# Hash attention and a Strassen SwiGLU block on one core: sums in another bank, weight words four pieces ahead, later gates, key before query

## The chip, the core and the metric

The kernel runs on one core of a Trainium2 chip. Five engines work beside each other, each in the order of its own queue: PE (TensorE, matrix products), DVE (VectorE), ACT (ScalarE), POOL (GpSimd, here the issuer of most transfers) and SP (SyncE, issuer of the others). The metric is device microseconds (us) of one execution.

## The reference

```python
def _attn_ref(q, k, v, proj):            # (4, 8, 768, 64), proj (64, 6)
    q_bucket = sum over 6 bits of (q @ proj > 0) * 2**bit
    k_bucket = the same of k
    scores = where(q_bucket == k_bucket, q @ k.T / 8, -1e9)
    attn = softmax(scores)               # with 1e-9 added to the sum
    return attn @ v

def _moe_ref(x, w_gate, w_val, w_out):   # (3072, 512), (512, 1536) twice, (1536, 512)
    g = x @ w_gate
    return (g * sigmoid(g) * (x @ w_val)) @ w_out
```

The attention's output, with its 8 heads side by side, is the x of the second block. Inputs are float32, apart from the three weights: these come as 64-bit doubles, as two 32-bit words each, and the kernel turns them into float32 itself.

## The kernel before

**Attention.** A batch has 4 pairs of heads; 4 batches make 16 pairs. A pair is done in two halves of 384 queries. I call such a half of a pair a unit and number the units 0 to 31; units 0 to 7 are the first batch's. In a unit `score` (L464) does six chunks of 128 keys for two heads: a float32 product of 64 rows, and a bfloat16 product of hash signs added on top in the same bank, which pushes pairs of unlike hash far down. ACT evicts each with an exponential (L467) into a ring of six tiles. `attend` (L476) multiplies them with the values into one bank of PSUM that has a pool of its own (`av_ps`, one buffer), and ACT copies it out (L480). `add` (L487, L491) sums the exponentials on DVE, `norm` (L501) adds up over the keys with a product by ones into a bank of the common pool, and DVE does a reciprocal (L504) and two more operations (L506, L507). The common pool `ps` has seven banks in rotation, for scores, transposes, hashes, sums and the feed-forward's products.

Ahead of a pair its queries and keys are transposed and hashed (`front`): in the first batch by PE (L388, L405), with ACT as evictor; later by DVE's block transposes (L431) and small hash products (L413). For pair 0 the order of these steps is written out by hand in `front`, and the first five of the eight are done before the first score.

**Weights.** 36 pieces of 128 x 512 doubles are brought in (`load_words`, L261), scaled by two ACT instructions (`scale_to`, L286 and L287) and put together on DVE in three steps (`narrow`, L303, L305, L308). Of each block of four pieces `form` makes, with eight DVE steps (L337), the combinations that Strassen's method wants, and writes them to a scratch in HBM (L330, L332, L339); `bring` (L322) reads them back when they are used. All of this is one generator, `preparing`, and `prepare_on(n)` takes n DVE steps from it at chosen places in the program. `load_words(i)` is called at the end of piece i and issues the loads of the next ones: up to four ahead for the first twelve pieces, three ahead afterwards. The words live in five tiles inside the hidden layer's buffer, idle at that time, for the first twelve pieces, and then in three tiles. `scale_ahead` lets ACT scale up to three (later two) pieces ahead. Piece 0 also has a check of the word order, with five DVE instructions more (L282 to L285, L300, L310).

**Feed-forward.** Once a batch's attention is complete, its feed-forward is cut into parts (`atoms`), which are put behind the attention of the next batch's units, about fourteen to a unit. An up stage (`both`) has seven Strassen products for the gate and seven for the value in turn (L533), on six banks named a, b and c. The first three are copied out by ACT (L591); for the later ones DVE adds the bank to what is there (L537). Then the gate: a tanh on ACT (L519), a first DVE step (L520), and for the value branch a second (L524), each of them one part after the product. Beside each part, 0.7 DVE steps of `preparing` and one `scale_ahead` are done. The down stage (`down_strassen`) does likewise with banks named po.

Each engine's queue has the order in which these calls are written out: nothing reorders them later.

Of the kernel before, what the change touches and what calls it, by code (L numbers as in the profile page):

```python
# [18 lines left out]
def kernel(  # L19
# [219 lines left out]


    words = {}
    EARLY = 12

    def as_words(t):
        return t.bitcast(I32).rearrange("p (f w) -> p f w", w=2)

    spare = hid.rearrange("p a b f q -> p (a b f q)")
    spare = [as_words(spare[:, i * 2 * PIECE : (i + 1) * 2 * PIECE]) for i in range(5)]
    beside = as_words(part(2 * PIECE, at=down_at + 8 * BL))

    def load_words(done, queue=nc.gpsimd):
        for i in range(len(words), len(pieces)):
            if i - done > (4 if i < EARLY else 3):
                break
            if i < EARLY:
                words[i] = spare[i % 5]
            elif i % 3 == 2:
                words[i] = beside
            else:
                words[i] = wraw.tile([P, PIECE, 2], I32, tag="words", name="words")  # L260
# [4 lines left out]
    bits_a, bits_b = (formed[x].rearrange("p n m -> p (n m)").bitcast(I32)[:, 0:PIECE]  # L265
                      for x in range(2))

    def scale_to(count):

        free = NJ * (progress["blocks"] + 2)
        if free >= 2 * NJ * DF // PIECE:
            free = len(pieces)
        for i in range(progress["scaled"], min(count, free, len(pieces))):
            t, w = words[i], pieces[i][0]
            top = t.rearrange("p f w -> p (f w)").bitcast(U16)
            top = top.rearrange("p (f w) -> p f w", w=4)[:, :, 1]
            if i == 0:

# [5 lines left out]
            nc.scalar.activation(w, t[:, :, 1].bitcast(FP32), AF.Copy, scale=2.0**-112)  # L286
            nc.scalar.activation(t[:, :, 0], top, AF.Copy, scale=2.0**-13 * (1 + 2.0**-17))  # L287
            progress["scaled"] = i + 1

    def scale_ahead():  # L290
        i = progress["piece"]
        scale_to(i + (3 if i < EARLY - 2 else 2))

    def narrow(i):
# [3 lines left out]
        wi = w.bitcast(I32)  # L298
        if i == 0:
            nc.vector.tensor_tensor(bits_b.bitcast(FP32), bits_a, lo, op=ALU.not_equal)  # L300
        scale_to(i + 1)
# [6 lines left out]
        nc.vector.tensor_tensor(wi, wi, lo, op=ALU.add)  # L308
        if i == 0:
            nc.vector.scalar_tensor_tensor(out=w, in0=bits_b.bitcast(FP32), scalar=1e4, in1=w,  # L310
                                           op0=ALU.mult, op1=ALU.add)
        progress["piece"] = i + 1
# [67 lines left out]
    def front(n):  # L380
# [158 lines left out]
    def up_strassen(x, b, first):  # L539
# [14 lines left out]
        def both(i):  # L554
# [4 lines left out]
            now = [{}, {}]  # L559
            later = {}  # L560

# [6 lines left out]
            def step(at):  # L568
# [34 lines left out]
                if at == 13:  # L603
                    later.pop(14)()

# [100 lines left out]

    prepare_pair(5)
    finish(rest)
    N = len(units)
    credit = ahead = 0.0  # L710
    for u in range(0, N, NCH):
# [41 lines left out]
        credit += 14 if n < 2 * NP else 15.75  # L753
        end = True
        while atoms and (credit > 0 or not end):
# [48 lines left out]
```

The softmax here doesn't subtract the row's maximum and nothing guards it: scores larger than these inputs give would overflow.

## Time and profile before

| what | before |
|---|---|
| time, median of 3 runs | 1030.21 us (1028.72 to 1030.33) |
| span of the profiled run | 1028.6 us |
| ACT busy | 418.8 us, 41% |
| POOL busy | 99.3 us, 10% |
| moved by DMA | 99.90 MB, mean 97 GB/s |

A line of the groups gives source line, engine, operation, output and input, count, busy time and mean, and then the idle time of the engine just before these instructions with what ended it:

```profile
L504 DVE RECIPROCAL r<-sum 128x384 f32<-128x384 f32 x32 | 81.7, 2554 | 27.1 <-PE sum L501 27.1
L467 ACT ACTIVATE A<-sc 128x384 f32<-128x384 f32 x256 | 105.9, 492 | 7.9 <-PE sc L464 7.8
L591 ACT COPY c<-up 128x384 f32<-128x384 f32 x72 | 34.4, 478 | 70.9 <-PE up L533 70.7
```

The first of them: 32 reciprocals of 2554 ns each, before which DVE idled for 27.1 us in all until the sums of PE were there. Idle time of an engine that isn't the bottleneck costs nothing. The row of 40 slices puts the work in time; a slice is 25.7 us:

```profile
DVE  5999987869895445565656472565656451525521
ACT  6776647365452413544352421534435201232200
```

### The profile page before, as it was taken

To read this page: it belongs to the slowest core of one execution; us is meant where nothing else is said; L and a number is where in the kernel's file an instruction comes from. 1 tells how busy PE (TensorE), PEld (TensorE's weight loads), DVE (VectorE), ACT (ScalarE), POOL (GpSimd) and SP (SyncE) were. 2 spreads that over 40 slices of the span, in tenths; PEclk is the share of its full clock that TensorE was granted. 3 is DMA by queue.
4 is the path that set the end of the run, shared out by engine and by line. 5 is a ranking of instruction groups with operands and counts; after the bars stand their busy time and mean duration, and the time that the engine had idled before them with its cause. 6 is when DMAs were issued, how large, how long until landed. Compare 5 with 4: busy or idle time off the path is not lost.

```text
span 1028.6 us, 12425 instructions
## 1 busy us (share of the span) xinstructions
PE 1014.7 (99%) x4597; PEld 610.6 (59%) x4597; DVE 624.5 (61%) x1012; ACT 418.8 (41%) x905; POOL 99.3 (10%) x192
## 2 busy tenths in 40 slices
PE   9999999999999999999999999999999999999998
PEld 4444455555557775555556677555555787555687
DVE  5999987869895445565656472565656451525521
ACT  6776647365452413544352421534435201232200
POOL 2212022321100000000000000000000000101000
PEclk9999999999999999999999999999999999999999
DMA  7656485744622114242321203233222000333101
GB/s 212 196 163 201 120 216 203 212 162 156 172 72 52 37 31 107 72 103 82 84 81 37 62 21 93 59 82 95 72 72 72 21 21 31 109 97 113 31 26 36
DMA packets 113884, 99.90 MB, mean 97 GB/s; under 512 B 86976, under 2 KB 97216, under 8 KB 113824
## 3 DMA queue, kind: packets, MB, share of 16 engines
q0 software_dynamic: 19104, 73.28, 21.7%
q1 hardware_dynamic: 93920, 25.64, 11.3%
q8 instruction: 36, 0.59, 0.2%
q10 hardware_dynamic: 800, 0.20, 0.1%
q14 instruction: 24, 0.20, 0.1%
HBM read 81.79 MB, written 17.30 MB: 96 GB/s over the span
## 4 chain that ended last, share of the span: by engine, by line
PE 81%; DVE 10%; issue 4%; DMA 3%; ACT 2%; POOL 1%; DVEq 0%; POOLq 0%
PE up L533 36%; PE po L533 21%; PE sc L464 11%; PE av L476 9%; DVE acc L491 2%; DMA words<-in_moe_w_out_dram 2%; DVE r L504 2%; PE sum L501 1%; DVE room L305 1%; PE hps L413 1%; DVE room L337 1%; DVE room L308 1%; ACT A L467 1%; PE hps L405 1%; DVE room L303 1%
## 5 line engine op out<-in xcount | busy, mean ns | idle before, releaser
L533 PE MATMUL up<-xT,room 128*128 128x384 f32 x768 | 263.5, 489 | 0.0
L533 PEld LDWEIGHTS up<-xT,room 128*128 128x128 f32 x768 | 143.9, 190 | 109.7 <-issue 15.2
L533 PE MATMUL up<-xc,room 128*128 128x384 f32 x576 | 198.3, 487 | 2.0 <-ACT hid L591 1.5
L464 PE MATMUL sc<-qT,kT 64*128 64x384 f32 x768 | 164.3, 498 | 7.3 <-DVE e L506 3.3
L533 PEld LDWEIGHTS up<-xc,room 128*128 128x128 f32 x576 | 109.0, 190 | 79.8 <-ACT hid L591 2.8
L537 DVE TENSOR_TENSOR c<-c,up 128x384 f32<-128x384 f32 x72 | 39.8, 552 | 151.9 <-PE up L533 151.9
L491 DVE TENSOR_TENSOR acc<-acc,A 128x768 f32<-128x768 f32 x128 | 122.7, 958 | 14.6 <-ACT A L467 1.6
L322 POOL DMA_DIRECT2D room<-ram x96 | 52.0, 542 | 671.9 <-PE up L533 662.4
L467 ACT ACTIVATE A<-sc 128x384 f32<-128x384 f32 x256 | 105.9, 492 | 7.9 <-PE sc L464 7.8
L464 PEld LDWEIGHTS sc<-qT,kT 64*128 64x128 f32 x768 | 69.6, 188 | 62.9 <-issue 45.5
L661 ACT COPY o<-po 128x256 f32<-128x256 f32 x48 | 17.9, 372 | 199.2 <-PE po L533 199.1
L504 DVE RECIPROCAL r<-sum 128x384 f32<-128x384 f32 x32 | 81.7, 2554 | 27.1 <-PE sum L501 27.1
L476 PE MATMUL av<-A,vraw 128*64 128x386 f32 x512 | 88.4, 487 | 0.0
L519 ACT ACTIVATE th<-c 128x384 f32<-128x384 f32 x72 | 37.6, 522 | 104.4 <-DVE c L537 104.2
L537 DVE TENSOR_TENSOR o<-o,po 128x256 f32<-128x256 f32 x36 | 15.2, 421 | 102.2 <-PE po L533 61.1
L467 ACT ACTIVATE room<-sc 128x384 f32<-128x384 f32 x128 | 54.3, 488 | 38.6 <-PE sc L464 38.3
L533 PE MATMUL po<-wo,hid 128*128 128x256 f32 x288 | 66.9, 382 | 0.0
L464 PE MATMUL sc<-qb,kb 64*128 64x384 bf16 x384 | 66.7, 324 | 0.2 <-DVE kb L400 0.2
L533 PE MATMUL po<-wo,room 128*128 128x256 f32 x288 | 66.3, 380 | 0.0
L533 PE MATMUL po<-room,hid 128*128 128x256 f32 x288 | 66.1, 379 | 0.0
L476 PEld LDWEIGHTS av<-A,vraw 128*64 128x64 f32 x512 | 36.8, 137 | 46.2 <-issue 45.3
L591 ACT COPY c<-up 128x384 f32<-128x384 f32 x72 | 34.4, 478 | 70.9 <-PE up L533 70.7
(113 smaller groups left out, 1041.3 us busy)
## 6 DMA issues: line engine op xcount, KB each, us to landing
room<-ram POOLq DMA_DIRECT2D x48, 512.0 KB, 4.7
room<-ram POOLq DMA_DIRECT2D x48, 384.0 KB, 3.9
vraw<-in_v_dram SPq DMA_DIRECT2D x16, 384.0 KB, 3.2
ram<-room POOLq DMA_DIRECT2D x12, 512.0 KB, 4.1
out_dram<-o SPq DMA_DIRECT2D x48, 128.0 KB, 1.7
qraw<-in_q_dram SPq DMA_DIRECT2D x48, 96.0 KB, 3.2
kraw<-in_k_dram SPq DMA_DIRECT2D x46, 96.0 KB, 3.4
words<-in_moe_w_out_dram POOLq DMA_DIRECT2D x8, 512.0 KB, 4.7
```

Of the source, the lines that this page charges most:

```text
L303: nc.vector.tensor_single_scalar(wi, wi, 3, op=ALU.logical_shift_left)
L322: nc.gpsimd.dma_start(places[k % 2][:, PARTS[go], :], ram[k % NG][:, PARTS[go], :])
L464: nc.tensor.matmul(sc[h], x["k", n][rows, ks], x["q", n][rows, qs], start=start, stop=not start)
L467: nc.scalar.activation(weights(u)[:, h, 0:HQ], sc[h], AF.Exp, scale=SCALE)
L476: nc.tensor.matmul(ps[h * D : (h + 1) * D, 0:AW], raws["v", n][:, h, c, :], a[:, h, :], start=c == 0, stop=c == NCH - 1)
L491: nc.vector.tensor_tensor(acc[n, half], acc[n, half], a[:, :, 0:HQ], op=ALU.add)
L504: nc.vector.reciprocal(r, ps[:, 0:HQ])
L519: nc.scalar.activation(th, g, AF.Tanh, scale=0.5)
L533: nc.tensor.matmul(ps, a, x, start=start and i == 0, stop=i == len(pairs_) - 1, skip_group_check=True)
L537: nc.vector.tensor_tensor(o, a, b, op=op)
L591: nc.scalar.copy(tile_of(g, spot), c)
L661: nc.scalar.copy(o, c)
```

## The change

It has five parts. The sums of the first batch's units go into the value product's bank instead of one of the seven. Words are loaded four pieces ahead throughout and scaled three ahead, in more tiles that lie in space idle at that time: the front and then the back of the hidden layer's buffer, and then the staging area; in the feed-forward's units the scaling is done only beside the parts after the fifth, and one preparation step beside each of the first ten parts. In the first batch four of the eight preparation steps of a unit move behind the reciprocal. The gate's second step, and its first, come two parts after the product instead of one. For pair 0 the key's first half is transposed and hashed ahead of the query's, and its second half behind the first score. The check of piece 0 is dropped. The purpose is to take waits out of the queues of ACT and DVE and to free PSUM banks of the rotation.

```diff
-    EARLY = 12
-    spare = hid.rearrange("p a b f q -> p (a b f q)")
-    spare = [as_words(spare[:, i * 2 * PIECE : (i + 1) * 2 * PIECE]) for i in range(5)]
-    beside = as_words(part(2 * PIECE, at=down_at + 8 * BL))
+    spots = [hid[:, half, m].rearrange("p f q -> p (f q)") for half in range(2) for m in range(2)]
+    early = [as_words(t[:, 0 : 2 * PIECE]) for t in spots]
+    early.append(as_words(part(2 * PIECE, at=down_at + 8 * BL)))
+    middle = [as_words(t[:, NFP // 2 * HQ : NFP // 2 * HQ + 2 * PIECE]) for t in spots]
+    late = [as_words(part(2 * PIECE, at=stage_at + i * 2 * PIECE)) for i in range(4)]
+
+    def words_tile(i):
+        if i < 12:
+            return early[i % 5]
+        if i < 24 and i % 6 < 4:
+            return middle[i % 6]
+        if i >= 24 and i % 6 not in (2, 3):
+            return late[i % 6 // 4 * 2 + i % 2]
+        return wraw.tile([P, PIECE, 2], I32, tag="words", name="words")
...
-            if i - done > (4 if i < EARLY else 3):
+            if i - done > 4:
                 break
...
-            if i == 0:
-                nc.vector.tensor_single_scalar(bits_a, t[:, :, 0], 29, op=ALU.logical_shift_right)
-                nc.vector.tensor_scalar(bits_b, t[:, :, 0], scalar1=28, scalar2=1,
-                                        op0=ALU.logical_shift_right, op1=ALU.bitwise_and)
-                nc.vector.tensor_tensor(bits_a, bits_a, bits_b, op=ALU.add)
...
-        scale_to(i + (3 if i < EARLY - 2 else 2))
+        scale_to(i + 3)
...
-            return [turns[2], turns[0], turns[1], hashes[2], hashes[0], hashes[1], turns[3],
+            return [turns[0], turns[2], hashes[0], hashes[2], turns[1], hashes[1], turns[3],
                     hashes[3]]
...
-        ps = bank("sum")
+        ps = av_ps.tile([P, 512], FP32, tag="av", name="sum") if b == 0 else bank("sum")
...
+                while later and later[0][0] <= at:
+                    later.pop(0)[1]()
                 if n >= 3 and g == 0:
-                    later[at + 1] = gate(tile_of(0, spot) if n == 6 else c, c)
+                    then = gate(tile_of(0, spot) if n == 6 else c, c)
                 elif n >= 3:
-                    later[at + 1] = lambda: gated(hidden(f + spot[0], spot[1]), now[0][spot], c)
-                if at in later:
-                    later.pop(at)()
+                    then = lambda: gated(hidden(f + spot[0], spot[1]), now[0][spot], c)
+                if n >= 3:
+                    later.append((at + (1 if n == 6 else 2), then))
...
-    prepare_pair(5)
+    prepare_pair(4)
...
-            if u == 0 and c in (1, 2, 4):
+            if u == 0 and c in (0, 1, 2, 4):
...
-        prepare_on(2 if u == LATE else 6)
+        prepare_on(2)
         norm(u + NCH - 1)
+        prepare_on(0 if u == LATE else 4)
...
             atom()
-            ahead += 0.7 * size
-            prepare_on(int(ahead))
-            ahead %= 1
-            scale_ahead()
+            part += size
+            if part < 11:
+                prepare_on(size)
+            if part > 5:
+                scale_ahead()
```

More of the change, by code (lines that the diff above doesn't have):

```diff
@@ L241 @@
     words = {}
-    EARLY = 12
     def as_words(t):
         return t.bitcast(I32).rearrange("p (f w) -> p f w", w=2)
-    spare = hid.rearrange("p a b f q -> p (a b f q)")
-    spare = [as_words(spare[:, i * 2 * PIECE : (i + 1) * 2 * PIECE]) for i in range(5)]
-    beside = as_words(part(2 * PIECE, at=down_at + 8 * BL))
+    spots = [hid[:, half, m].rearrange("p f q -> p (f q)") for half in range(2) for m in range(2)]
[11 more added lines that the diff above has]
+        return wraw.tile([P, PIECE, 2], I32, tag="words", name="words")
     def load_words(done, queue=nc.gpsimd):
         for i in range(len(words), len(pieces)):
-            if i - done > (4 if i < EARLY else 3):
+            if i - done > 4:
                 break
[L255 to L260, printed above, removed]
+            words[i] = words_tile(i)
             queue.dma_start(words[i].rearrange("p f w -> p (f w)"), pieces[i][1])
     progress = {"late": False, "piece": 0, "scaled": 0, "blocks": 0}
-    bits_a, bits_b = (formed[x].rearrange("p n m -> p (n m)").bitcast(I32)[:, 0:PIECE]
-                      for x in range(2))
     def scale_to(count):
@@ L298, in narrow @@
         wi = w.bitcast(I32)
-        if i == 0:
-            nc.vector.tensor_tensor(bits_b.bitcast(FP32), bits_a, lo, op=ALU.not_equal)
         scale_to(i + 1)
@@ L308, in narrow @@
         nc.vector.tensor_tensor(wi, wi, lo, op=ALU.add)
-        if i == 0:
-            nc.vector.scalar_tensor_tensor(out=w, in0=bits_b.bitcast(FP32), scalar=1e4, in1=w,
-                                           op0=ALU.mult, op1=ALU.add)
         progress["piece"] = i + 1
@@ L559, in both @@
             now = [{}, {}]
-            later = {}
+            later = []
             def tile_of(g, spot):
@@ L594, in step @@
                     c = my[spot]
+                while later and later[0][0] <= at:
+                    later.pop(0)[1]()
                 if n >= 3 and g == 0:
-                    later[at + 1] = gate(tile_of(0, spot) if n == 6 else c, c)
+                    then = gate(tile_of(0, spot) if n == 6 else c, c)
                 elif n >= 3:
-                    later[at + 1] = lambda: gated(hidden(f + spot[0], spot[1]), now[0][spot], c)
-                if at in later:
-                    later.pop(at)()
+                    then = lambda: gated(hidden(f + spot[0], spot[1]), now[0][spot], c)
+                if n >= 3:
+                    later.append((at + (1 if n == 6 else 2), then))
                 if n in (3, 6):
                     bring(k0 + 2 + g, n // 6)
-                if at == 13:
-                    later.pop(14)()
+                while at == 13 and later:
+                    later.pop(0)[1]()
             for n in range(2 * NB):
@@ L705, in finish @@
             todo.pop(0)()
-    prepare_pair(5)
+    prepare_pair(4)
     finish(rest)
     N = len(units)
-    credit = ahead = 0.0
+    credit = 0.0
     for u in range(0, N, NCH):
@@ L754 @@
         end = True
+        part = 0
         while atoms and (credit > 0 or not end):
```

## The prediction

> **What bounds the kernel now.** I number the units (pair, half) 0 to 31: 0 to 7 hold the first batch's attention, and from unit 8 on each unit also carries fourteen parts of the feed-forward. The page's first part seems to leave nothing:
>
> ```profile
> PE 1014.7 (99%) x4597; PEld 610.6 (59%) x4597; DVE 624.5 (61%) x1012; ACT 418.8 (41%) x905; POOL 99.3 (10%) x192
> ```
>
> But a matmul's end is modelled, so I went by starts, in the chain of waits. From 300 us on the same groups come back at fixed distances:
>
> ```profile
> 399.54 5.04 PE sc L464 x36
> ...
> 428.51 5.04 PE sc L464 x36
> ...
> 456.50 5.05 PE sc L464 x36
> ```
>
> One unit with a hash takes 28.97 us, one without 27.99, and the chain is PE alone. There is nothing to win there. Before 300 us it is otherwise. Windows of the first batch give the vector engine nearly all of its time:
>
> ```profile
> 25.00:50.00 25.00, 23.08 (x138) 10.52 (x136) 23.70 (x35) 18.06 (x39) 6.79 (x11) 1.00 0.58 191
> 50.00:75.00 25.00, 24.17 (x146) 11.15 (x142) 23.66 (x35) 19.23 (x42) 3.65 (x6) 1.00 0.56 166
> 75.00:100.00 25.00, 24.93 (x152) 11.88 (x152) 23.76 (x33) 15.88 (x36) 4.72 (x8) 1.00 0.66 206
> ```
>
> (Columns after the length: PE, PEld, DVE, ACT, POOL busy, clock, DMA share, GB/s.) In its timeline DVE has no gap from 17.2 to 135.8 us; PE only now and then waits for it. From 120 to 300 us the stage is mixed. Its score groups start at 142.45, 173.76, 202.35, 236.10, 264.96 and 296.01, after the sum of unit 8 at 122.44. At the steady distances this stretch of 173.57 would be 18.9 (sum and up products) + 3 x 28.97 + 2 x 27.99 = 161.8. So **11.8 us are lost there**. Where, the PE timeline shows:
>
> ```profile
> 167.11 1.56 PE L533 MATMUL up<-xc,room 128*128 128x384 f32 x4 [0.93 <-ACT hid L591]
> ...
> 208.15 1.01 PE L464 MATMUL sc<-qT,kT 64*128 64x384 f32 x1 [2.47 <-ACT room L467]
> ```
>
> and the chain around the second says why:
>
> ```profile
> 196.58 0.51 POOL room L322
> 197.10 9.39 DMA words<-in_moe_w_out_dram
> 206.52 0.66 ACT wo L286
> 207.18 0.54 ACT words L287
> 208.15 4.10 PE sc L464 x11
> ```
>
> A weight piece issued at 197.10 landed 9.39 us later; the scaling that reads it (L286) stood ahead of the unit's exponentials in ScalarE's queue, so these and PE stood too. The waits confirm a habit, not an accident:
>
> ```profile
> ACT wo L286 <- DMA words<-in_moe_w_out_dram: 14.4, 6, 4.9
> ...
> ACT room L286 <- DMA words<-in_moe_w_gate_dram: 6.9, 2, 4.6
> ```
>
> (Columns: us in total, times, longest.) That is 21.3 us of ScalarE's queue held by late words; two like rows for the third buffer add 4.0.
>
> **What the Trainium skill says.** "DMA: Bandwidth & Descriptors", Anatomy of one DMA, fits a GpSimd transfer as about 2.0 us plus bytes / 436e3: 3.2 us for 512 KB, as an estimate. This trace has 3.4 at best, 4.5 in the median and 9.4 at worst for the pieces, so the fit is a floor only; I use the trace. "TensorE: Matmul & The Clock Gate", Part 1, says a PE left idle for a window of some 3.4 us loses its clock. The trace agrees in kind: the window 205 to 210, with the wait of 2.47, was granted 0.76, the next one 0.90. "PSUM — Partial Sum Buffer", Specifications, gives 8 banks per partition; the kernel owns all, seven in rotation and one for the value product, and the up products hold six of the seven. So a bank held long is a stall.
>
> **The change part by part.**
>
> *Check removed (piece 0).* Five vector instructions go: 0.42 + 0.42 + 0.69 + 0.69 + 0.69 = 2.9 us from their rows at 18.10 to 22.21, in the stretch where DVE is the bound. But the same edit sequence puts only four preparation steps ahead of the reciprocal. DVE ends unit 0's adds at 18.1, does four steps (0.42 + 0.69 + 0.69 + 0.42, about 2.3) by 20.4, then waits for the sum, which PE ends at about 22.5 and, PE being continuous from 9 us, hardly sooner. Some 2 us become idle. **Net 0.9 us.**
>
> *Key first.* Three 128x128 transposes (0.45 us) and one copy (0.43) move behind the first scores. PE's work before the first sum is the same and PE is without gaps there, bar 0.19 at 9.15. I take 0; up to 0.3.
>
> *Sums in the value bank; four steps before, four after.* The stalls of the fifth or sixth score group go (1.56, 0.36, 0.22, 0.61, 0.59 us on the release of the sum's bank after the reciprocal). Worth nothing by themselves: DVE does the same eight steps per unit, its mean unit from 28.92 to 116.78 is 87.86 / 7 = 12.55, PE's own work about 12.0. PE will wait for the adds at the sum instead. New waits: the sum needs the copy of the value product (0.48). PE does 0.87 to 1.49 us of transposes or hashes in between, so it hides, except in units whose ScalarE does three scalings (3.6 us) first, where 74.14 (copy ends) meets 74.25 (sum starts): 0 to 0.1. And the next value product needs the reciprocal: it starts at most 1.9 us after the sum's end and takes 2.5; the value product is 5.7 or more behind. Hidden. DVE's new wait for the sum: adds end, four steps and the sign scaling take 1.6 to 2.9, the sum 0.9. Hidden while DVE is the bound.
>
> *Words four ahead, in more buffers; scaling only after the fifth part.* The count of scalings is the same, 36 of 1.2 us (two instructions of about 0.69, less their overlap); only their place changes. In the order of the built programs ScalarE now does all six copies of the up products (L591) before a block of two to four scalings, then the tanh. The copies free what PE's parts 4 to 9 accumulate on, so the 0.93 at 167.11 and the 0.60 at 253.16 go. No scaling stands last before the exponentials in units 10 and 12 any more (it did at 206.52 and 266.42). Lag from a piece's issue to its scaling, by the order: four parts or more, 4 x 1.3 = 5.2 us, against 4.5 in the median and up to 9.4. In unit 10, where the query and key loads in small packets fall together with the ram traffic (window 195 to 200: DMA share 1.22), I expect a landing 2 to 4 us late ahead of the second tanh; behind it stand the gates, which free the banks of the next scores.
>
> *Gate's second step two parts later; one preparation step beside each of the first ten parts and none beside the last four (it was 0.7 beside each of fourteen).* DVE waited 1.88 us (138.26) and 2.46 us (168.83) for a tanh; with one part more (1.3 us) between them most of it is filled by work that is there anyway. The last gates come sooner. In unit 8 DVE takes 23.2 us from the end of the adds (122.0) to the release of the first gate's bank (145.17); less the 1.88 idle, with one step of 0.42 more by the order, 21.7. From 121.1 this gives 142.8. PE, 1.9 earlier than before by the items above, asks for it at 142.6 to 143: 0 to 0.4 left, I take 0.4.
>
> By stall, before and left: end of unit 8's parts 1.1 and 0.1; its gates 1.15 and 0.4; unit 9's copies 1.1 and 0; next scores 0.6 and 0.5; words before exponentials and the low clock 4.8 and 1.8; copies at 253.16 0.9 and 0.1; words at 266.42 2.1 and 0.5; a new stall in unit 11, whose scalings had found their place before: 0.5. Saved 11.75 - 3.9 = 7.85. With 0.9 from the first batch: **8.7 us, so 1021.5**. From 300 us on I expect nothing.
>
> **Rivals.** *All lost time comes back*: if the words always land in time, 11.8 + 0.9 = 12.7, **1017.5**. For it: five parts of slack; against: a DMA share of 0.75 already in the window 175 to 200, and 30.6 MB (175 us at 175 GB/s) squeezed into less time. *DVE becomes the bound of the mixed stage*: its busy time in 125 to 300 is 146.5 of 175; with ten preparation steps in the first ten parts ahead of the sums that PE waits for, only the word waits ahead of exponentials come back, about 3.5: **1026.7**. *Slower*: scalings in a row of three or four, ahead of every tanh, each block held by one landing of 9.4 with a lag of 5.2, cost 4.2 in units 9 to 12, 16.8 against the 10.7 lost there now, so 0.9 - 6.1: **1035.4**. Against it: the median landing is 4.5, and tanh has its own slack of two parts.
>
> **How the numbers follow.** My forecast (1019 to 1024) 0.58; nearly all back 0.12; DVE or words still hold it (1024 to 1028.1) 0.17; within 0.2% 0.06; slower 0.07. Faster is the sum of the first three, 0.87. The range 1017.5 to 1027.5 leaves out the slower cases, no change and the edges of the two side cases.
>
> **What would show it.** Right: score groups 28 to 29 us apart from 142 on; hardly any wait of the exponentials or of L591's successor for words; the clock 1.00 in all slices; sum of unit 8 about 1 us earlier, not 5; DVE without gaps in the first batch but for 2 us near 20.5; the same distances after 300. Wrong: a first batch shorter by over 2 us (then PE's bank stalls did count), or tanh standing behind scalings that wait for words in units 10 and 11.

## The result, and the profile after

The changed kernel takes **1023.0 us** (median of 4 runs, 1022.44 to 1023.69) beside 1030.27 us for the kernel before (4 runs, 1028.72 to 1031.61): a ratio of 0.993, 95% interval 0.9913 to 0.9947. That is faster by 0.7%, inside the range and 1.5 us above the forecast of 1021.5. The spans of the profiled runs are 1021.6 and 1028.6 us. Line numbers of the changed kernel lie 8 or 9 below those of before: L455 are the scores, L458 the exponentials, L493 the sum, L496 the reciprocal, L482 the adds, L525 the up products, L282 and L283 the scaling of words, L297, L299 and L302 their narrowing, L267 their load, L511 the tanh, L583 the copies.

The first part of the page again tells nothing:

```profile
PE 1011.9 (99%) x4597; PEld 609.5 (60%) x4597; DVE 621.5 (61%) x1007; ACT 419.4 (41%) x905; POOL 99.2 (10%) x192
```

The chain of waits does. Its shares by engine now read

```profile
PE 92%; DVE 3%; ACT 2%; issue 2%; DMA 0%; ACTq 0%; DVEq 0%; POOLq 0%
```

where PE had 81% and DVE 10% before. From 300 us on the chain has the same distances as before (28.97 us and 27.99 to 28.06):

```profile
392.57 5.04 PE sc L455 x36
...
421.54 5.04 PE sc L455 x36
...
449.52 5.04 PE sc L455 x36
```

The windows of the first batch still show VectorE (third figure after the length) as the bound:

```profile
25.00:50.00 25.00, 24.52 (x152) 11.70 (x148) 23.32 (x35) 19.39 (x43) 6.82 (x11) 1.00 0.57 162
50.00:75.00 25.00, 23.93 (x148) 11.46 (x146) 23.80 (x35) 18.63 (x42) 3.66 (x6) 1.00 0.66 200
75.00:100.00 25.00, 24.76 (x154) 11.91 (x152) 23.72 (x35) 17.29 (x40) 5.51 (x10) 1.00 0.67 215
```

The gain lies in the mixed stage, as forecast. ScalarE's waits for words, 25 us in four rows before, are one row (us in total, times, longest):

```profile
ACT wo L282 <- DMA words<-in_moe_w_out_dram: 4.8, 1, 4.8
```

and these are the long waits of TensorE that are left between the first batch and 300 us, from its timeline (the longest of the others is 0.18 us):

```profile
121.68 0.87 PE L493 MATMUL sum<-acc,ones 128*64 128x384 f32 x4 [1.76 <-DVE acc L482]
122.48 7.12 PE L525 MATMUL up<-xT,room 128*128 128x384 f32 x16
...
170.72 1.56 PE L525 MATMUL up<-xc,room 128*128 128x384 f32 x4 [0.54 <-DVE hid L529]
...
204.95 0.59 PE L455 MATMUL sc<-qT,kT 64*128 64x384 f32 x1 [1.09 <-DVE c L512]
```

The second of these lines is one to stop at. Sixteen up products took 7.12 us, where a later row of sixteen (183.02) takes 5.43. The windows say why; the figure after the five engines is the granted clock:

```profile
120.00:125.00 5.00, 3.32 (x8) 1.58 (x9) 4.90 (x10) 0.47 (x1) 0.00 (x0) 0.77 0.00 1
125.00:130.00 5.00, 5.00 (x15) 2.96 (x14) 4.93 (x6) 1.80 (x4) 0.53 (x1) 0.89 0.28 78
```

Behind the wait of 1.76 us TensorE ran at a lower clock and took 1.7 us more for these products.

To compare kernels I use one measure throughout: what each unit takes beyond its steady distance, from the starts of the sum of unit 8 and of the score groups of units 9 to 14 (steady: 18.9 for unit 8, then 28.97, 27.99, 28.97, 27.99, 28.97). The kernels named E are the experiments below; E5 moves the very sum from which the measure starts and is left out. The profiles of before, changed, E3, E4, E6 and E13 are of executions in which the clock fell somewhere, the others of executions in which it did not.

| us lost in unit | 8 | 9 | 10 | 11 | 12 | 13 | sum |
|---|---|---|---|---|---|---|---|
| before | 1.1 | 2.3 | 0.6 | 4.8 | 0.9 | 2.1 | 11.8 |
| changed | 1.9 | 0.8 | 1.1 | 2.1 | 0 | 0 | 5.8 |
| E1 sum's bank back | 0.2 | 1.7 | 1.1 | 2.4 | 0 | 0 | 5.3 |
| E2 place back | 0.2 | 2.4 | 1.6 | 0 | 0 | 0 | 4.1 |
| E3 three tiles, three ahead | 0.3 | 2.0 | 1.1 | 2.4 | 0.1 | 7.2 | 13.0 |
| E4 gate one part later | 1.9 | 2.0 | 0 | 3.5 | 0.8 | 0 | 8.2 |
| E6 fillers | 0.2 | 1.7 | 1.1 | 4.3 | 0 | 0 | 7.3 |
| E7 piece 26 moved | 0.2 | 1.7 | 1.1 | 0 | 0 | 0 | 3.0 |
| E10 three ahead | 0.2 | 1.0 | 0.8 | 0 | 0.1 | 0 | 2.1 |
| E13 three ahead, place back | 0.2 | 2.2 | 1.0 | 4.5 | 0 | 0 | 7.9 |
| E14 before with tiles | 0.1 | 1.8 | 0.6 | 1.6 | 0 | 0.4 | 4.5 |
| E15 E10 with check and order back | 0.2 | 1.0 | 0.7 | 0 | 0.1 | 0 | 2.0 |
| E16 E10 with four tiles | 0.2 | 1.0 | 0.7 | 0 | 0.1 | 1.2 | 3.2 |

The lower clock costs less than the 1.7 us above. E1, E6 and E7, whose clock stayed up behind the sum of unit 8, lose 1.7 us in unit 9, where the changed kernel loses 0.8: units 8 and 9 together take 2.7 us with the lower clock there and 1.9 without.

Of the 7.0 us between the spans, 0.76 come by the sum of unit 8 (121.68, before 122.44), 5.97 in the mixed stage, 0.3 later. For the first batch a finer measure is needed, since VectorE's first add starts anywhere from 11.75 to 12.65 us in these profiles. From that start to the sum of unit 8 there are 110.42 us in the kernel before and 110.38 in E14, which has its first batch; 109.33 in the changed kernel, and 109.31 to 109.35 in the seven others with the same first batch and no filler. So the first batch is worth 1.09 us, and a few hundredths can be told.

The experiments were timed in three groups, each beside the kernel before and each on another chip: E1 to E4, E5 to E10, E13 to E16. At full clock the kernel before took 1029.5, 1029.3 and 1027.7 us there (last section), so a time of the third group is not comparable with one of the others to better than 1.6 us; the ratios are the better guide.

### The profile page after: what moved, and what is told of

It is laid out like the page before. It is cut to its first block, busy times and chain, and to the rows that moved or that the text cites. A ratio compares the mean times of both kernels' runs of the same rounds, so it can differ in the third digit from the quotient of the medians.

```text
span 1021.6 us, 12400 instructions
## 1 busy us (share of the span) xinstructions
PE 1011.9 (99%) x4597; PEld 609.5 (60%) x4597; DVE 621.5 (61%) x1007; ACT 419.4 (41%) x905; POOL 99.2 (10%) x192
## 4 chain that ended last, share of the span: by engine, by line
PE 92%; DVE 3%; ACT 2%; issue 2%; DMA 0%; ACTq 0%; DVEq 0%; POOLq 0%
PE up L525 40%; PE po L525 21%; PE sc L455 14%; PE av L467 11%; PE sum L493 2%; PE hps L396 1%; DVE acc L482 1%; PE hps L404 1%; DMA words<-in_moe_w_out_dram 0%; ACT room L282 0%; PE tps L379 0%; DVE r L496 0%; PE idle L134 0%; ACT A L458 0%; ACT hid L283 0%
## 5 line engine op out<-in xcount | busy, mean ns | idle before, releaser
L525 PE MATMUL up<-xT,room 128*128 128x384 f32 x768 | 265.2, 492 | 0.0
L525 PEld LDWEIGHTS up<-xT,room 128*128 128x128 f32 x768 | 144.7, 191 | 110.6 <-issue 16.9
L525 PE MATMUL up<-xc,room 128*128 128x384 f32 x576 | 197.8, 486 | 0.5 <-DVE hid L529 0.5
L455 PE MATMUL sc<-qT,kT 64*128 64x384 f32 x768 | 160.8, 493 | 1.3 <-DVE c L512 1.3
L525 PEld LDWEIGHTS up<-xc,room 128*128 128x128 f32 x576 | 109.4, 190 | 77.2 <-DVE hid L529 1.2
L482 DVE TENSOR_TENSOR acc<-acc,A 128x768 f32<-128x768 f32 x128 | 122.7, 958 | 15.7 <-ACT A L458 1.9
L458 ACT ACTIVATE A<-sc 128x384 f32<-128x384 f32 x256 | 105.5, 490 | 3.0 <-PE sc L455 3.0
L455 PEld LDWEIGHTS sc<-qT,kT 64*128 64x128 f32 x768 | 67.7, 186 | 54.6 <-issue 48.9
L496 DVE RECIPROCAL r<-sum 128x384 f32<-128x384 f32 x32 | 81.8, 2555 | 30.4 <-PE sum L493 30.3
L655 ACT COPY o<-po 128x256 f32<-128x256 f32 x48 | 17.9, 373 | 199.1 <-PE po L525 199.0
L511 ACT ACTIVATE th<-c 128x384 f32<-128x384 f32 x72 | 37.6, 523 | 109.7 <-DVE c L512 91.1
L458 ACT ACTIVATE room<-sc 128x384 f32<-128x384 f32 x128 | 54.5, 489 | 43.0 <-PE sc L455 41.9
L583 ACT COPY c<-up 128x384 f32<-128x384 f32 x72 | 34.5, 479 | 82.1 <-PE up L525 81.9
L525 PE MATMUL po<-wo,hid 128*128 128x256 f32 x288 | 66.9, 382 | 0.0
L525 PE MATMUL po<-wo,room 128*128 128x256 f32 x288 | 66.3, 380 | 0.0
L525 PE MATMUL po<-room,hid 128*128 128x256 f32 x288 | 66.1, 379 | 0.0
L455 PE MATMUL sc<-qb,kb 64*128 64x384 bf16 x384 | 64.8, 323 | 0.0
```

The costliest lines, as they stand in the source:

```text
L455: nc.tensor.matmul(sc[h], x["k", n][rows, ks], x["q", n][rows, qs], start=start, stop=not start)
L458: nc.scalar.activation(weights(u)[:, h, 0:HQ], sc[h], AF.Exp, scale=SCALE)
L482: nc.vector.tensor_tensor(acc[n, half], acc[n, half], a[:, :, 0:HQ], op=ALU.add)
L496: nc.vector.reciprocal(r, ps[:, 0:HQ])
L511: nc.scalar.activation(th, g, AF.Tanh, scale=0.5)
L525: nc.tensor.matmul(ps, a, x, start=start and i == 0, stop=i == len(pairs_) - 1, skip_group_check=True)
```

## The experiments

My theory after the result was that of the prediction: the place of the scalings in ScalarE's queue carries the gain. The rivals were the distance of the loads and the tiles they go into. The first four kernels take parts of the change back.

**E1, the sum in the rotation of banks.**

```diff
-        ps = av_ps.tile([P, 512], FP32, tag="av", name="sum") if b == 0 else bank("sum")
+        ps = bank("sum")
```

> The changed kernel, but with all sums in the rotation of seven banks again, as before the change. Theory (the vector engine is the bound of the first batch, the bank only moves PE's waits from the score groups to the sum): the sum of unit 8 starts within 0.4 us of the 121.7 of the changed kernel, PE's waits come back at the fifth or sixth score group, and as none of them is long the clock may stay at full speed behind that sum, so the time is the same or up to 1.7 us less: 1021.3 to 1023.3. Rival (PE's stalls on the bank were part of the first batch's length): 2 to 3 us more, 1025 to 1026.

Measured: 1023.17 us (1022.88 to 1023.38), ratio 0.9938 (0.9922 to 0.9955): by the median as the changed kernel, as the theory said. The sum of unit 8 starts at 121.70, but the first add at 11.75: 109.95 us by the finer measure, 0.62 more than in the changed kernel. Of the five stalls of this kind that the kernel before had, one is back,

```profile
PE sc L455 <- DVE e L498: 0.7, 1, 0.7
```

and behind it VectorE, the bound, waits 0.48 us for a sum, where it had no gap:

```profile
111.16 2.56 DVE L496 RECIPROCAL r<-sum 128x384 f32<-128x384 f32 x1 [0.48 <-PE sum L493]
```

So the bank is worth 0.6 us, too little for the medians to tell.

**E2, the place of scalings and preparation steps as before; loads and tiles as changed.**

```diff
-            part += size
-            if part < 11:
-                prepare_on(size)
-            if part > 5:
-                scale_ahead()
+            ahead += 0.7 * size
+            prepare_on(int(ahead))
+            ahead %= 1
+            scale_ahead()
```

> The changed kernel, with loads four ahead and the new tiles, but preparation (0.7 step beside each part) and scaling (beside every part) placed as before the change. Theory (the place of the scalings in ScalarE's queue, and of the preparation in the vector engine's, made most of the gain from 122 to 296 us): 4 to 6 us come back, 1027 to 1029, and copies of the up products or exponentials stand behind scalings that wait for words. Rival (it is the loads further ahead that count, wherever the scaling stands): at most 2 us more, below 1025.

Measured: 1021.92 us (1021.56 to 1026.65), ratio 0.9936 (0.9913 to 0.996). My theory falls: with four ahead in the new tiles the place is not what carries the gain; undoing it costs nothing that these runs can tell.

**E3, words in three tiles, three ahead, at the new places.**

```diff
-        if i < 24 and i % 6 < 4:
-            return middle[i % 6]
-        if i >= 24 and i % 6 not in (2, 3):
-            return late[i % 6 // 4 * 2 + i % 2]
+        if i % 3 == 2:
+            return early[4]
...
-            if i - done > 4:
+            if i - done > (4 if i < 12 else 3):
...
-        scale_to(i + 3)
+        scale_to(i + (3 if i < 10 else 2))
```

> The changed kernel, with its places for scaling and preparation, but words loaded three ahead and scaled two ahead from the thirteenth piece on, in three tiles as before. Theory (place counts most): 1 to 3 us more, 1024 to 1026, as more scalings are forced at the start of a piece ahead of the sixth part. Rival (distance of the loads counts most): 4 us or more, 1027 and above.

Measured: 1030.22 us (20 runs), ratio 0.9994 (0.9985 to 1.0003). The whole gain is gone. Unit 13 alone loses 7.2 us, as much as the sums in the table differ by; the smaller differences in the other units cancel out. ScalarE's timeline (start, length, instruction, idle before it) shows a loop there:

```profile
254.43 0.68 ACT L280 ACTIVATE wo<-words 128x512 f32<-128x512 f32 x1 [1.61 <-DMA words<-in_moe_w_out_dram]
...
258.69 0.68 ACT L280 ACTIVATE wo<-words 128x512 f32<-128x512 f32 x1 [2.60 <-DMA words<-in_moe_w_out_dram]
...
262.94 0.66 ACT L280 ACTIVATE wo<-room 128x512 f32<-128x512 f32 x1 [2.61 <-DMA room<-in_moe_w_out_dram]
```

A piece each 4.26 us, with a wait for its words before each. GpSimd's timeline has the other half:

```profile
249.06 0.53 POOL L265 DMA_DIRECT2D words<-in_moe_w_out_dram  x1 [1.10 <-DVE wo L300]
251.68 0.53 POOL L265 DMA_DIRECT2D words<-in_moe_w_out_dram  x1 [2.10 <-DVE wo L300]
...
254.67 0.53 POOL L265 DMA_DIRECT2D room<-in_moe_w_out_dram  x1 [1.94 <-DVE wo L300]
```

Each load waits for the narrowing (L300 here) of the piece that lies in its tile: with as many tiles as pieces ahead, load, scaling and narrowing run one after another. TensorE then waits once, for long, and its clock falls to 0.53:

```profile
266.25 1.00 PE L453 MATMUL sc<-qT,kT 64*128 64x384 f32 x1 [3.39 <-DVE c L510]
```

```profile
265.00:270.00 5.00, 3.75 (x14) 3.00 (x16) 3.55 (x6) 2.78 (x8) 0.00 (x0) 0.53 0.62 118
270.00:275.00 5.00, 5.00 (x27) 2.60 (x25) 3.48 (x5) 2.16 (x6) 0.00 (x0) 0.79 0.00 0
```

**E4, the gate's two steps one part after the product, as before.** (In the changed kernel they come two parts after it, except behind the last of the seven products.)

```diff
-                    later.append((at + (1 if n == 6 else 2), then))
+                    later.append((at + 1, then))
```

> The changed kernel, but with the gate's steps one part after the product, as before. Theory: the vector engine waits for a tanh once more in units 8 to 12, of which PE feels 0.5 to 1.5 us in all: 1023.5 to 1024.5. Rival (the two waits of 3.1 us for a tanh behind a row of scalings are there with either distance and decide): within 0.3 us of 1023.0.

Measured: 1024.42 us, ratio 0.9953 (0.9938 to 0.9967), 1.4 us more than the changed kernel. As expected; a wait of 1.76 us for a product of VectorE at 170.92 takes the place of the 0.54 at 170.72.

The next four ask what is left in the changed kernel, and part distance from tiles.

**E5, the sum of unit 8 behind two parts of the feed-forward.**

```diff
-        norm(u + NCH - 1)
+        if u != LATE:
+            norm(u + NCH - 1)
...
             part += size
+            if u == LATE and part == 2:
+                norm(u + NCH - 1)
```

> The changed kernel, but the sum of the ninth unit (unit 8) stands behind the first two parts of the feed-forward product, so that TensorE has work while VectorE ends its row of running sums. In the changed kernel TensorE idles 1.76 us there, and the granted clock is 0.77 and 0.89 in the ten microseconds behind it, which makes the sixteen matmul pairs behind it take 7.12 instead of 5.43 us (1.7 us). Theory (that gathered wait and the clock behind it still cost): both go, the clock stands at 1.00 from 115 to 145 us, and the time falls by 2.0 to 3.5 us, to 1019.5 to 1021.0. Rival (the lower clock is not due to the wait, or the wait comes back as one for the gates of the same unit): 1022.5 to 1023.5.

Measured: 1023.08 us, ratio 0.9924 (0.991 to 0.9938): no gain; the rival holds. The wait is gone at the sum and back in the same unit, for the gates:

```profile
122.48 0.87 PE L493 MATMUL sum<-acc,ones 128*64 128x384 f32 x4
...
137.79 2.85 PE L525 MATMUL up<-xc,room 128*128 128x384 f32 x8 [1.35 <-DVE c L529]
```

VectorE is the bound up to the end of unit 8, so it doesn't matter where TensorE waits for it, except for the clock.

**E6, fillers ahead of that sum.**

```diff
+        if u == LATE:
+            ps = bank("idle")
+            t = sides["k", 0]
+            for _ in range(8):
+                nc.tensor.matmul(ps, t[:, 0:P], t[:, 0:512], start=True, stop=True)
         norm(u + NCH - 1)
```

> The changed kernel with eight bf16 matmuls of no use, into a bank of the rotation, ahead of the same sum: TensorE is busy in the wait, but the sum starts no earlier. It tells the clock apart from the wait. Theory (TensorE's idleness lowers the clock behind it): the clock stays at 1.00 from 120 to 130 us, the wait's 1.76 us are still lost, and the time is 1021.2 to 1021.9 (1.7 us off, less what the fillers overrun). Rival (the clock falls there for another cause): 0.77 and 0.89 as before, 1023.0 to 1023.6. Two other kernels with the same wait of 1.76 us showed no lower clock in the one execution profiled, so a third way is that the clock falls only in some executions: then the median moves by less than 1 us.

Measured: 1022.59 us, ratio 0.9922 (0.9907 to 0.9937): the third way. In the profiled run the clock is 1.00 behind the sum, but it fell elsewhere, behind waits of 0.34 and 1.09 us:

```profile
205.00:210.00 5.00, 4.95 (x22) 3.63 (x22) 3.24 (x4) 2.44 (x6) 0.00 (x0) 0.66 0.59 187
```

Since E2, E3, E7, E10, E13, E15 and E16 have the wait of 1.76 us without fillers and a clock of 1.00 behind it in their profiles, E6 can't show that the fillers kept it up. That the lower clock behind this wait comes in some executions only is what it leaves; the mean clock of each run, below, says the same.

**E7, another tile for piece 26.**

```diff
+        if i == 26:
+            return early[4]
         if i < 24 and i % 6 < 4:
```

> The changed kernel with another tile for one piece of words, the 27th (26), whose load there waits for the last tanh of the weights' stage (issued at 195.46, landed 4.7 us later, ScalarE waits 4.84 us, VectorE 3.07, TensorE 1.09 at 204.95 us). Theory (the time at which a load may be issued sets the waits that are left): the load is issued some 8 us earlier, the three waits go, the score groups of units 11 and 12 stand 29.0 to 30.0 us apart instead of 31.02, and the time falls by 1.0 to 2.0 us, to 1021.0 to 1022.0. Rival (VectorE is behind anyhow in this unit): the waits change their name, 1022.6 to 1023.4.

Measured: 1020.4 us, ratio 0.9898 (0.9884 to 0.9912): 2.6 us less than the changed kernel, more than expected. There, GpSimd, ScalarE and VectorE read one after the other

```profile
195.46 0.54 POOL L267 DMA_DIRECT2D words<-in_moe_w_out_dram  x1 [10.64 <-ACT th L511]
195.99 1.05 POOL L313 DMA_DIRECT2D room<-ram  x2
```

```profile
200.21 0.67 ACT L282 ACTIVATE wo<-words 128x512 f32<-128x512 f32 x1 [4.84 <-DMA words<-in_moe_w_out_dram]
```

```profile
201.88 0.56 DVE L512 SCALAR_TENSOR_TENSOR c<-th,c 128x384 f32<-128x384 f32 x1 [3.07 <-ACT th L511]
```

The load stood for 10.64 us at the head of GpSimd's queue, with two reads of combinations (`bring`) behind it. For the first 8.5 us its tile still held piece 22, whose narrowing ended at 193.34; the last thing that it waited for, by the profile, was a tanh that ended at 195.37, and why that one was in its way is not shown. "TensorE: Matmul & The Clock Gate" of the Trainium skill, Architectural detail, says that GpSimd's queue is strictly first in, first out for each of its cores; the second line agrees, for both transfers start when the load is out. In E7 the load goes out at 185.02, and the three waits are gone; unit 11 loses nothing.

```profile
185.02 0.57 POOL L269 DMA_DIRECT2D room<-in_moe_w_out_dram  x1 [1.44 <-issue]
```

**E10, the changed kernel's tiles and places, but loads three ahead and scaling two ahead.**

```diff
-            if i - done > 4:
+            if i - done > (4 if i < 12 else 3):
...
-        scale_to(i + 3)
+        scale_to(i + (3 if i < 10 else 2))
```

> The changed kernel with its own tiles for the words and its own places of the scaling, but loads only three pieces ahead and scaling only two ahead from the thirteenth piece on. The kernel with three tiles, three ahead, took 1030.2 and lost 7.1 us at one place, unit 12 to 13, where each load was issued only when a piece had been narrowed out of its tile (4.26 us from scaling to scaling: landing 2.6, scaling 0.6, narrowing the rest). Theory A (the distance counts): the same loop stands, 1028 to 1031. Theory B (free tiles count, since a load into a tile long free is issued as soon as GpSimd reaches it, whatever the distance): 1023 to 1025.

Measured: **1019.64 us** (1019.61 to 1020.05), ratio 0.9892 (0.9877 to 0.9908), 3.4 us less than the changed kernel and better than theory B asked. At these places the fourth piece ahead is worth less than nothing; E3 differs from this kernel in its tiles alone and takes 10.6 us more. All that TensorE waits for is on three rows; the second is at the start, and only the first matters:

```profile
PE sum L493 <- DVE acc L482: 3.3, 3, 1.8
PE idle L134 <- DVE kb L131: 1.3, 1, 1.3
PE sum L493 <- ACT qT L382: 0.2, 1, 0.2
```

The landings did not get shorter: the loads of the output weights into the pool's tiles take 6.5 us in the median here, 4.7 in the kernel before. They start earlier: that of piece 25 at 182.63, in the kernel before at 197.10.

The edit moves two things, though, and for piece 26, the one that the changed kernel waits for, it is not the load that counts. It goes out at 193.44, only 2 us earlier than there, but the scaling of this piece now stands in the next unit, 17.9 us later, and waits for nothing:

```profile
218.06 0.68 ACT L282 ACTIVATE wo<-words 128x512 f32<-128x512 f32 x1
```

The two distances, of loads and of scaling, were not tried apart.

The last four test what the tiles are worth, on this kernel and on the kernel before.

**E13, E10 with the old places too** (E10's edit and E2's), so that of the words' schedule only the tiles are new.

> The changed kernel with its tiles for the words, but everything else of the words' schedule as in the kernel before: loads three pieces ahead from the thirteenth piece on, scaling two ahead, a scaling and 0.7 of a preparation step beside each of the fourteen parts. Theory (the tiles carry the gain: a load into a tile long free goes out when GpSimd reaches it, and not when the piece three back has been narrowed): 1019.5 to 1022. Rival (distance, place and tiles work together, each alone is worth little): 1025 or more.

Measured: 1024.67 us (1022.58 to 1025.68), ratio 0.9959 (0.9944 to 0.9975). Neither. Against E10, which has the same tiles and distances, the place is worth 5 to 7 us (5.0 by the medians, 6.9 by the ratios). Against E2, which has the same tiles and places, loads four ahead and scaling three ahead seem worth some 2.5 us (2.4 by the ratios, whose intervals overlap; 3.8 in the table): at the old places the larger distance looks like a gain, at the new ones it is a loss. The stall is of the very kind that the prediction described, a scaling that waits for its words ahead of the exponentials (L458):

```profile
204.56 0.66 ACT L282 ACTIVATE wo<-room 128x512 f32<-128x512 f32 x1 [4.34 <-DMA room<-in_moe_w_out_dram]
205.13 0.63 ACT L283 ACTIVATE room<-room 128x512 int32<-128x512 uint16 x1
205.67 1.61 ACT L458 ACTIVATE room<-sc 128x384 f32<-128x384 f32 x4
```

with a wait of 1.95 us for TensorE at 206.19 and a clock of 0.76 behind it. The load, of piece 25, had been issued at 194.63 and landed some 9.9 us later. It had not waited for its tile but behind a read of combinations:

```profile
194.09 0.54 POOL L313 DMA_DIRECT2D room<-ram  x1 [2.34 <-issue]
194.63 0.53 POOL L267 DMA_DIRECT2D room<-in_moe_w_out_dram  x1
```

In E2, with four ahead, the load of this piece stands ahead of such reads and goes out at 186.59.

**E14, the kernel before with the new tiles and nothing else** (the definitions of the tiles and `words_tile` are the change's own).

```diff
-            if i < EARLY:
-                words[i] = spare[i % 5]
-            elif i % 3 == 2:
-                words[i] = beside
-            else:
-                words[i] = wraw.tile([P, PIECE, 2], I32, tag="words", name="words")
+            words[i] = words_tile(i)
```

> The kernel before, with the changed kernel's tiles for the words and nothing else of the change (its distances, the places of its scalings, the check of the first piece, the bank of the sums, the gates one part later, and the order of the first key and query all stay). Theory (tiles): the waits of ScalarE on words fall from 25 to under 8 us, the mixed stage from 122 to 296 us loses 6 to 8 us of its 11.8, and the time is 1022.5 to 1024.5; what is left to the best kernel so far (1019.6) is the check, 0.9, and the gates, 1.4. Rival: under 3 us off, 1027.5 or more.

Measured: 1022.45 us beside 1028.14 for the kernel before on that chip, ratio 0.9943 (0.9926 to 0.996). ScalarE's waits for words fell to 8.5 us, slightly more than expected:

```profile
ACT wo L292 <- DMA room<-in_moe_w_out_dram: 5.2, 2, 3.1
ACT room L292 <- DMA hid<-in_moe_w_gate_dram: 2.6, 1, 2.6
ACT room L292 <- DMA words<-in_moe_w_val_dram: 0.7, 1, 0.7
```

The longest of these waits is for piece 25 again, whose load now goes out at 195.78, still behind a read. Otherwise the theory holds: the mixed stage loses 4.5 instead of 11.8 us. The time falls by 5.7 us in the median and by 4.9 at full clock (1027.7 to 1022.8), less than the 7.3 of the table, where the profile before has a lower clock behind its wait of 2.47 us. By ratio, one part of the change does most of what the whole does (0.993). The parts don't simply add: E13 is this kernel with the rest of the change apart from distance and place (bank, gates, check, key's order, the four steps behind the reciprocal), and on the same chip it took 2.2 us longer, 0.4 at full clock.

**E15, E10 with the check of piece 0 and the order query before key back.**

```diff
+            if i == 0:
+                nc.vector.tensor_single_scalar(bits_a, t[:, :, 0], 29, op=ALU.logical_shift_right)
...
-            return [turns[0], turns[2], hashes[0], hashes[2], turns[1], hashes[1], turns[3],
+            return [turns[2], turns[0], turns[1], hashes[2], hashes[0], hashes[1], turns[3],
```

> The kernel with the loads three ahead in the new tiles (1019.64), with the check of the first piece and the order query before key put back: what the change did to the first batch outside the sums' bank. Theory (first batch bound by VectorE, 2.9 us of check less some 2 us that are idle without it, the order worth nothing): the sum of unit 8 starts 0.7 to 1.1 us later, and the time is 1020.2 to 1021.0. Rivals: the check in full, 1022.5; nothing (it is hidden), 1019.4 to 1019.9.

Measured: 1019.28 us (1018.73 to 1020.15), ratio 0.991 (0.9894 to 0.9925); the sum of unit 8 starts at 121.29, 109.49 us after the first add, 0.16 more than without the check. Theory falls, the second rival holds: next to nothing. VectorE's timeline shows the check fitting mostly into idle time. In the changed kernel,

```profile
20.33 0.42 DVE L297 TENSOR_SCALAR room<-room 128x512 int32<-128x512 int32 x1
22.95 2.56 DVE L496 RECIPROCAL r<-sum 128x384 f32<-128x384 f32 x1 [2.20 <-PE sum L493]
```

and in E15, with the same steps and the check ahead of it,

```profile
22.59 0.42 DVE L307 TENSOR_SCALAR room<-room 128x512 int32<-128x512 int32 x1
23.00 2.56 DVE L509 RECIPROCAL r<-sum 128x384 f32<-128x384 f32 x1
```

Counted from the first add (12.35 and 11.80), the reciprocal starts only 0.60 us later in E15, since the check fills the 2.20 us that were idle. A second idle piece of 0.52 us, at 43.71 in the changed kernel, is gone too, so that 0.16 are left of the 0.60. The times of E15 and E10, from two chips, can't tell so little.

**E16, E10 with four tiles from piece 12 on instead of six.**

```diff
-        if i < 24 and i % 6 < 4:
-            return middle[i % 6]
-        if i >= 24 and i % 6 not in (2, 3):
-            return late[i % 6 // 4 * 2 + i % 2]
+        if i % 4 == 0:
+            return early[4]
+        if i % 4 == 1:
+            return middle[0] if i < 24 else late[0]
```

> The same kernel with the loads three ahead, but with only four tiles for the words from the thirteenth piece on, one more than the distance, where the changed kernel has six and the kernel before three. Theory (the tile must be free one piece before its load comes up): four are enough, 1019.5 to 1021.0, and no wait of ScalarE on words over 2 us. Rival (every tile more gives slack): between the two, 1023 to 1027, with the wait of 2.6 us per piece in unit 12 partly back.

Measured: 1020.83 us (1020.21 to 1022.16), ratio 0.9927 (0.9909 to 0.9944). The time is as expected, 1.55 us above E15 on the same chip, which has six tiles. One tile more than the distance brings nearly all; but one wait of ScalarE for words of 3.1 us is left, over the 2 us I had allowed, and unit 13 loses 1.2 us that E10 does not.

## Why the prediction was right, and where it was not

**Right: where the time was lost and how much could come back.** The bound of the mixed stage, late words ahead of work in ScalarE's queue, is what went away; the sum over all units was forecast at 3.9 us left of 11.75, and 5.8 of 11.8 are left. No rival came: not all of it back, not VectorE as the bound of the mixed stage (1026.7), not slower. The distances after 300 us did not change, as said.

How near the number came is in part luck: 8.7 us were forecast and 7.3 came, but what was put down to the place came mostly with the tiles, and units 8 to 10, where 2.8 us too little were forecast, were partly made up by units 12 and 13 and the new stall in unit 11, where 1.1 us too much were.

**Wrong: which edit does it.** The prediction put the saving of 7.85 us down to the place of the scalings. E2 undoes the place and loses nothing; E14 brings in only the tiles and gains 7.3 us in the mixed stage by the profiles, 4.9 to 5.7 in time. The prediction had read the lag from issue to scaling off the order of instructions, "four parts or more", as if a load were issued where it stands in the program. It is issued when its tile is free: with three tiles and three ahead that is the narrowing three pieces back (E3), and with four ahead it was so again for piece 26 (E7). It is also issued only when what stands ahead of it in GpSimd's queue is out (piece 25 in E13 and E14). Place (E13 against E10, 5 to 7 us) and tiles (E3 against E10, 10.6 us) aren't rivals but the two ends of one lag: tile and queue set the earliest issue, the place the latest need, and a stall comes where the landing, 9.9 us in E13, doesn't fit between. Distance moves both ends, the load's place in the queue and the scaling's: four ahead seems to help at the old places (E2 against E13) and hurt at the new ones (the changed kernel against E10). (The median landing of 4.5 us that the prediction took is that of the mixed stage; over all 34 loads from GpSimd it is 4.8.)

**Sizes, unit by unit** (numbers from the table; the forecast is what was said to be left):

- Unit 8: 0.1 forecast, 1.9 left in the profile; 0.2 in the kernels without the lower clock there. The prediction had noted the clock behind a wait of 2.47 us but not that its own new wait for the adds, ahead of the sum, could bring it. As unit 9 gets back half of it, that is some 0.8 us of the 1.9 by which the sum is off, not 1.7.
- Units 9 and 10: 0.4 (gates; copies 0) and 0.5 forecast, 0.8 and 1.1 left, and 1.7 in unit 9 where the clock stayed up. Too low.
- Unit 11, words ahead of exponentials: 1.8 forecast, 2.1 left. The size was right for a wrong reason: not a landing 2 to 4 us late in crowded queues (it took 4.7 us) but an issue 10.64 us late.
- Units 12 and 13: 0.6 forecast, nothing left; the extra 0.5 for unit 11 didn't come.

**The gates.** 0.75 us were put down to their later place at the end of unit 8 (1.15 to 0.4). E4 lost 1.4 us in the median, about twice that, and not there: in its profile as in that of the changed kernel, TensorE does not wait between the sum of unit 8 and the last products of unit 9, at 170.92.

**The first batch.** 0.9 us were forecast and 1.09 came, by other parts than said. The check is worth 0.16 (E15): 2.9 us of work went, and idle time of 2.20 and 0.52 us came in their place. The prediction had the first of these (about 2) and missed the second. The bank, "worth nothing by themselves", is worth 0.62 (E1), since a stall of TensorE there still reaches the bound, VectorE. If these parts add, some 0.3 us are left, and were not settled; the move of four steps behind the reciprocal was not tried alone. The zero for the key's order isn't contradicted: E15 starts its first add at 11.80, within the scatter of the others.

**What would show it.** The words' waits, the earlier sum and the distances after 300 us are as said. VectorE's gaps are as said but for the 0.52. Units 9 and 11 are 29.78 and 31.02 us long, not 28 to 29, and the clock was not 1.00 throughout (the page gives tenths, too coarse to show it). One of the signs against it came too, a tanh behind a scaling that waits for words, in unit 10 (the 3.07 us above), and it led to the faulty step.

## What to carry to other kernels

When a prefetched buffer arrives late, look first at when the load was issued and what it waited for: here the tile in which an earlier piece still lay, seen as a wait of the issuing queue, or the transfers ahead of it in that queue. Give a prefetch of n pieces at least n + 1 tiles (E16; n tiles made load, use and release run in a row, E3), and don't raise the distance beyond what the tiles allow, since the load then blocks the queue for others. Then tune the distance and the place of the consumer together, since the best of one depends on the other. The kernel with the best ratio, E10 (0.9892), is the change with loads and scaling one piece nearer; E7 (0.9898) can't be told from it.

## What the runs showed of the hardware that I had not expected

The granted clock behind waits of one to two microseconds differs between executions of the same kernel. The mean clock of the span was recorded for each run:

| kernel | runs at 1.000, mean | runs below, mean |
|---|---|---|
| before, beside E1 to E4 | 10, 1029.5 us | 13, 1032.0 us |
| before, beside E5 to E10 | 5, 1029.3 us | 6, 1031.8 us |
| before, beside E13 to E16 | 9, 1027.7 us | 3, 1031.0 us |
| changed | 2, 1022.5 us | 2, 1023.6 us |
| E13 | 3, 1023.2 us | 4, 1025.3 us |
| E3 | 1, 1027.9 us | 19, 1030.4 us |
| E7, E10 and E15 together | 15 | none |

In these rows the runs below took 1.0 to 3.3 us longer, and most of the spread of a kernel's times goes with it. At full clock the change is worth the same 7 us (1029.5 against 1022.5, of separate groups of runs), so the gain isn't made of it.

"TensorE: Matmul & The Clock Gate" of the Trainium skill, Part 1, says that the array turns cold after at least one idle window of about 3.4 us, and that the window runs freely, so that the moment of a change depends on its phase. That the outcome differs from run to run fits this; the phase itself is in no run here. The length doesn't fit: the clock fell behind waits of 1.76 us (changed kernel), 1.95 (E13), 2.47 (kernel before, where the prediction took it for agreement), and 0.34 and 1.09 in a row (E6), each well below 3.4, and it didn't in the profiles of seven other kernels with the same 1.76. What decides is open. E7, E10 and E15 have the wait of 1.76 us too, and none of their 15 runs was below, so it can't be the length of that wait alone.
